# Fewer and wider idle products on TensorE

## The chip, the core and the metric

The kernel runs on one core of a Trainium2 chip. The metric is the device time of one execution in microseconds. A core has five engines, each with an instruction queue of its own: TensorE (PE, matrix products; its weight loads are PEld), VectorE (DVE), ScalarE (ACT), GpSimd (POOL) and SyncE (SP, which issues most loads and stores). They wait for each other by semaphores.

## The reference

Attention over 4 batches and 8 heads of 768 positions and 64 columns, then a gated two-layer network on the 3072 rows of 512. Heads marked for retrieval see all earlier positions; the others see the first 4 and the last 64.

```python
scores = scale * np.matmul(q, k.transpose(0, 1, 3, 2))
mask = np.where(retr[0, :, 0, 0, None, None], full_mask, stream_mask)
scores = np.where(mask[None, :, :, :], scores, -1000000000.0)
a = np.exp(scores - np.max(scores, axis=-1, keepdims=True))
a = a / (np.sum(a, axis=-1, keepdims=True) + 1e-09)
x = np.matmul(a, v)            # then heads side by side: 3072 x 512
h = x @ w_in                   # 512 -> 2048
g = h * (1.0 / (1.0 + np.exp(-beta * h)))
out = g @ w_out                # 2048 -> 512
```

## The kernel before

The work is cut into eight units, one for each batch and half of the positions (384 rows). For a unit, queries and keys are loaded, cast to bf16 (tiles `c`), turned on TensorE against the identity (`transposes_of`, in the first two units one tensor and pair of heads at a time), copied to `QK`, multiplied to scores (`scores`, into PSUM tiles `sp`), passed through the exponential on ScalarE (tiles `es`, or `osb`) and masked. Sums of the exponentials and their products with v follow, the sums are inverted and spread, and the result `xT` (512 rows, 384 columns) goes through the network: `w_in`, a tanh form of the gate, `w_out`, a copy out of PSUM and a store.

All operations of all units are in one list, and `SEQUENCE` is the order in which they are issued, so each engine gets its instructions in that order. Loads go through SP's queue. The network of one unit runs beside the attention of the next, which keeps TensorE full from about 20 us on; before that only the first unit's attention is there.

In this first stretch the kernel issues idle products: matrix products whose results nobody reads, into PSUM that real work overwrites afterwards. `FILLS` names operations of the list by number and says how many idle products are issued ahead of the real ones; `fill_first` issues 25 at the very start. Operation 28 turns the first keys, 32 and 36 the keys of the second and fourth pair of heads; 45, 51, 54 and 60 are scores; 24 is the product that makes the rows of the first positions (`sink_rows`). The operand `blank` is a cleared piece of an `xT` tile, cleared on VectorE by the first instruction there. Ahead of transposes the PSUM tile is bf16, and there the idle product is a transpose of the identity.

```python
FILLS = {24: 4, 28: 8, 32: 1, 36: 1, 45: 5, 51: 7, 54: 5, 60: 1}
for i, f, e in plan.run():
    held["fill"] = FILLS.get(i, 0)
    f(e)
```

Of the kernel before, what the change touches and what calls it, by code (L numbers as in the profile page):

```python
# [8 lines left out]
F32 = mybir.dt.float32  # L9
BF16 = mybir.dt.bfloat16  # L10
# [9 lines left out]
NQ = 384  # L20
# [85 lines left out]
    return bass.AP(ap.tensor, ap.offset + offset, [list(ap.ap[0])] + dims)  # L106


FILLS = {24: 4, 28: 8, 32: 1, 36: 1, 45: 5, 51: 7, 54: 5, 60: 1}


class _Ordered:
# [60 lines left out]
def kernel(  # L173
# [14 lines left out]
    pe, dve, act, pool, sp = (_Ordered(tc, e) for e in (nc.tensor, nc.vector, nc.scalar, nc.gpsimd, nc.sync))  # L188
# [3 lines left out]
    NP = len(PAIRS)  # L192
# [4 lines left out]
    def tpool(name, bufs, space=None):  # L197
        kw = {} if space is None else {"space": space}
        return ctx.enter_context(tc.tile_pool(name=name, bufs=bufs, **kw))
# [11 lines left out]
    xp = tpool("xp", RINGS["xT"])  # L211
# [4 lines left out]
    ps = tpool("ps", 1, PSUM)  # L216
    dp = tpool("dram", 2, bass.MemoryType.DRAM)

    def bank(name):
        return ps.tile([128, 512], F32, name=f"b{plan.where['b', name]}")  # L220

    def banks(name):
        return ps.tile([128, 2, 512], F32, name=f"sp{plan.where['sp', name]}")
# [7 lines left out]
    ident = consts.tile([128, 128], BF16, name="ident")  # L231
# [11 lines left out]
    sel_c = consts.tile([128, 2, 8], F32, name="sel_c")  # L243
    sel_k3 = consts.tile([128, CK // 2], F32, name="sel_k3")
    low = consts.tile([128, 1], F32, name="low")
    blank = xp.tile([128, NP, NQ], BF16, name="xT")[:, 0, 0:128]
    one = consts.tile([128, 63], BF16, name="one")
    warm = consts.tile([128, 1], F32, name="warm")
    QK = [consts.tile([128, 2, NP, S], BF16, name=f"QK{par}") for par in range(2)]
# [216 lines left out]
    held = {}  # L466

    def sink_rows(b):

        t = bank((2 * b, "k"))  # L470
        fill(t[:, 0:128])
        pe.matmul(t[0:96, :], sink_sel, v_b[b][:, 0, :, :].rearrange("p h d -> p (h d)"), start=True, stop=True)
        held["sinks"] = t

# [53 lines left out]

    def fill(dst):
        for _ in range(held["fill"]):  # L530
            if dst.dtype == BF16:
                pe.transpose(dst, ident, ident)
            else:
                pe.matmul(dst, blank, blank, start=True, stop=True)

    def fill_first():
        held["fill"] = 25
        fill(bank("fill")[:, 0:128])

    def transposes(x, pi):  # L540
        t = ps.tile([128, 2, 512], BF16, name=f"b{plan.where['b', (x.n, 'T', pi)]}")
# [11 lines left out]
    def transposes_of(x, pi, i):  # L553
        t = ps.tile([128, 2, 512], BF16, name=f"b{plan.where['b', (x.n, 'T', pi, i)]}")
        x.ps["T", pi, i] = t[:, 0, 0:NQ].rearrange("p (t n) -> p t n", t=TU)
        c = x.ld[pi, "c"]
        fill(x.ps["T", pi, i][:, 0, :])
        for t in range(TU):
            pe.transpose(x.ps["T", pi, i][:, t, :], c[:, i, t * 128:(t + 1) * 128], ident)

# [122 lines left out]
    def piece(x, h, a, n):  # L683
        for (c, w, e) in x.work[h]:
            if c <= a and a + n <= c + w:
                return e[:, a - c:a - c + n]

    def scores(x, pi, ri, mixed=None):
# [5 lines left out]
        if lent(pi, ri, x.n):  # L694
            ps = [bank((x.n, pi, ri, i)) for i in range(2)]
        else:
            both = banks((x.n, pi, ri))
            ps = [both[:, i, :] for i in range(2)]
        if x.n == 0:
            fill(ps[0][:, 0:128])  # L700
        ops = [[], []]
        last = []
        nb, ne = NE[u] // SINK, NE[u]
# [7 lines left out]
        for i, half in enumerate(rounds[ri]):  # L711
            if half is None:
                continue
            if half[0][0] == "k":
                for g in range(NP):
                    p = min(g, NP - 2) + 1
# [36 lines left out]
            for h in dict.fromkeys(t[1] for t in half if t[0] in "sw"):  # L753
                pieces = [t for t in half if t[0] in "sw" and t[1] == h]
                q0 = 0 if pieces[0][0] == "w" else pieces[0][4]
                n = NQ if pieces[0][0] == "w" else sum(t[5] for t in pieces)
# [23 lines left out]
    def scores_mixed(x, bu):  # L780

        todo = []
        for pi, ri in bu:
            scores(x, pi, ri, todo)
        queues = {}
        for o in [o for r in todo for o in r]:
            row, col = (a.offset // a.ap[0][0] for a in (o[1], o[0]))
            queues.setdefault((row, col), []).append(o)
        at = dict.fromkeys(queues, 0)
        while queues:  # L790
            g = min(queues, key=lambda g: at[g])
            o = queues[g].pop(0)
            n = 1
            for d in o[2].ap[1:]:
                n *= d[1]
            at[g] += max(n, 64) + 6
            pe.matmul(o[0], o[1], o[2], start=True, stop=True)
            if not queues[g]:
                del queues[g]
# [86 lines left out]
    def sink_from(u):  # L886
        return 2 * W if u == 0 else 0
# [4 lines left out]
    def sums(x, part):  # L892
        if part == 0:
            x.sm = bank((x.n, "s"))
            if x.n == 0:
                fill(x.sm[:, 0:128])
        todo = [[] for _ in range(4)]
        heads = [h for pi in SUMS[part] for h in PAIRS[pi]]
        for c in range(CK):
            a = c * W  # L900
            g, s = PLACE[c]
            for h in heads:
                e8 = two[:, 1, 31 - h:63 - h] if c >= 4 else two[:, 0, 31 - 16 * s - h:63 - 16 * s - h]
                if RETR[h]:
                    todo[g] += [(e8, e[:, a - q0:a - q0 + W]) for (kb, q0, n, e) in x.work[h] if q0 <= a // 128 * 128 < q0 + n]
                else:
                    todo[g].append((e8, piece(x, h, a, W)))
            if part == len(SUMS) - 1 and a >= sink_from(x.u):
                todo[g].append((esel_k[:, 16 - 16 * s:48 - 16 * s], x.esk[0:96, a:a + W]))
        for r in range(max(len(w) for w in todo)):  # L910
            for g in range(4):
                if r < len(todo[g]):
                    l, e = todo[g][r]
                    pe.matmul(x.sm[32 * g:32 * g + 32, 0:W], l, e, start=(part == r == 0),
                              stop=(part == len(SUMS) - 1 and r == len(todo[g]) - 1))
# [105 lines left out]
    def moved(x, h):  # L1021
        return x.u and h == 6

    def pv(x, g):
        vb = v_b[x.b]
        ve = VE[x.b]
        o = banks((x.n, "v", g))
        if x.n == 0:
            fill(o[:, 0, 0:128])
        ops = [[], []]  # L1030
        nb = NE[x.u] // SINK
        for t in (2 * g, 2 * g + 1):

            for i, h in enumerate(XT[t] if x.n else (2 * t, 2 * t + 1)):
                dst = o[i * D:(i + 1) * D, t - 2 * g, :]
                todo = ops[i]
                if h in x.zero:
                    todo.append((W, dst[:, 0:W], x.vz[:, h, :] if h < H // 2 else x.vs[:, 0, h, :], x.zero[h], t, 0))
                if RETR[h]:

                    cut = 256 if moved(x, h) else NQ
                    for (kb, q0, n, e) in x.work[h]:
                        a = min(max(cut - q0, 0), n)
                        if a:
                            todo.append((a, dst[:, q0:q0 + a], vb[:, kb, h, :], e[:, 0:a], t, 0))
                        if a < n:
                            ops[1 - i].append((n - a, o[(1 - i) * D:(2 - i) * D, t - 2 * g, NQ + q0 + a - cut:NQ + q0 + n - cut],
                                               vb[:, kb, h, :], e[:, a:n], t, 0))
                else:
                    q0 = sink_from(x.u)  # L1050
                    for m in range(1 if h in x.zero else 0, CK):
                        if x.n < 2 and m * W == q0:
                            todo.append((NQ - q0, dst[:, q0:NQ], ve[0:96, h - 1, :], x.esk[0:96, q0:NQ], t, 0))
                        mg = CK * x.u + m
                        l = vb[:, (mg - 1) // 2, h, :] if mg % 2 else x.vs[:, m // 2, h, :]
                        todo.append((W, dst[:, m * W:(m + 1) * W], l, piece(x, h, m * W, W), t, int(x.n < 2 and not mg % 2)))
                    if x.n < 2:
                        continue
                    todo.append((NE[x.u], dst[:, 0:NQ].rearrange("d (c n) -> d c n", n=W)[:, CK - nb:, 0:SINK], ve[:, h - 1, :], x.edge[h], t, 0))
        todo = []  # L1060
        for late in range(2):
            at = [0, 0]
            queue = [[o for o in ops[i] if o[5] == late] for i in range(2)]
            while queue[0] or queue[1]:
                i = min((i for i in range(2) if queue[i]), key=lambda i: at[i])
                todo.append((i, *queue[i].pop(0)))
                at[i] += todo[-1][1]
        for k, (i, n, a, l, r, t, _) in enumerate(todo):
            same = [j for j, w in enumerate(todo) if w[0] == i and w[5] == t]
            pe.matmul(a, l, r, start=k == same[0], stop=k == same[-1], skip_group_check=True)  # L1070
        x.ps["v", g] = o
# [362 lines left out]
# [3 lines that stand above are left out]
# [35 lines left out]
```

## Time and profile before

| what | value |
|---|---|
| runs of the kernel | 229.29 us median of 3 (228.82 to 229.96) |
| span of the profiled execution, first to last instruction | 227.1 us |
| outside the span, median less span | 2.2 us |
| TensorE busy | 220.0 us, 97% of the span |
| ScalarE, VectorE, GpSimd busy | 144.4, 152.0, 97.1 us |
| mean granted clock of TensorE | 0.999 |

The runs were timed without the profiler, and the profiled execution has no time of its own beside its span; so the span is set against the median. A busy row of the profile gives when an instruction started and how long it took up to its modelled end; matrix products overlap, so the distance of their starts is the rate and the length is more than that. Names that the profile shows are those of tiles, without buffer numbers: `b` and `sp` are PSUM tiles, `c` the cast queries and keys, `xT` both the network's input and the idle operand, `ident` the identity. All instructions carry line 123, that of a helper, so they are told apart by their tiles.

### The profile page before, as it was taken

How to read it: one execution, taken by the hardware profiler on the slowest of the kernel's cores; microseconds unless marked ns; L12 is line 12 of the kernel's file. 1: busy time of each engine (PE TensorE's matmuls, PEld its weight loads, DVE VectorE, ACT ScalarE, POOL GpSimd, SP SyncE). 2: the span in 40 equal slices, each digit the busy share in tenths (PEclk: the TensorE clock that was granted, in tenths of full speed). 3: DMA queues.
4: the chain of work that ended last, by engine and by line, in shares of the span. 5: the costliest groups of instructions: out<-in, count | busy, mean ns of one | idle time of the engine just before them, and what ended most of it. 6: DMA issues, size and time to landing. Idle time of an engine off the chain costs nothing.

```text
span 227.1 us, 6564 instructions
## 1 busy us (share of the span) xinstructions
PE 220.0 (97%) x2595; PEld 127.2 (56%) x2595; DVE 152.0 (67%) x391; ACT 144.4 (64%) x244; POOL 97.1 (43%) x238
## 2 busy tenths in 40 slices
PE   7688999999999999999999999999999999999995
PEld 7564567664545565555654665465655555456543
DVE  5787988888292878856862668983796864157700
ACT  6899979886447488616786198318965665118620
POOL 5528966965978108749566293042800000000000
PEclk9999999999999999999999999999999999999999
DMA  6999999998999969999999996947801027021012
GB/s 185 283 321 369 242 343 349 371 335 217 233 205 244 213 131 235 270 176 208 267 219 189 202 214 192 219 26 178 188 0 46 4 89 200 3 92 46 3 46 92
DMA packets 84264, 42.28 MB, mean 186 GB/s; under 512 B 66042, under 2 KB 77002, under 8 KB 84234
## 3 DMA queue, kind: packets, MB, share of 16 engines
q1 hardware_dynamic: 83962, 41.67, 76.7%
q8 instruction: 20, 0.33, 0.6%
q10 hardware_dynamic: 272, 0.20, 0.3%
q14 instruction: 10, 0.08, 0.1%
HBM read 32.27 MB, written 6.37 MB: 170 GB/s over the span
## 4 chain that ended last, share of the span: by engine, by line
PE 87%; DMA 5%; DVE 3%; ACT 2%; SPq 1%; issue 1%; POOL 0%; ACTq 0%
PE b L123 77%; PE sp L123 10%; DMA vf<-in_v_dram 3%; DMA q2f<-in_q_dram 2%; DVE gT L123 1%; ACT t L123 1%; SPq L123 1%; ACT R L123 1%; DVE vs L123 1%; DVE xT L123 0%; ACT vb L123 0%; DVE QK L123 0%; POOL c L123 0%; DVE b L123 0%; DVE lo L123 0%
## 5 line engine op out<-in xcount | busy, mean ns | idle before, releaser
L123 PE MATMUL b<-xT,w_in 128*128 128x384 bf16 x512 | 89.9, 326 | 0.1
L123 PE MATMUL b<-w_out,gT 128*128 128x512 bf16 (+2 forms) x400 | 88.3, 371 | 0.0
L123 DVE SCALAR_TENSOR_TENSOR gT<-t,b 128x384 bf16<-128x384 f32 x128 | 68.5, 551 | 26.2 <-ACT t L123 22.5
L123 ACT ACTIVATE t<-b,beta_h 128x384 f32<-128x384 f32 x128 | 72.2, 586 | 18.3 <-PE b L123 9.7
L123 PEld LDWEIGHTS <-w_in 128*128 128x128 bf16 x512 | 48.6, 98 | 33.4 <-issue 0.6
L123 PEld LDWEIGHTS <-gT 128*128 128x128 bf16 x400 | 37.4, 98 | 40.9 <-issue 0.8
L123 ACT ACTIVATE es<-sp 128x1024 bf16<-128x1024 f32 (+2 forms) x44 | 41.2, 961 | 6.5 <-PE sp L123 6.0
L123 ACT ACTIVATE osb<-b 128x512 f32<-128x512 f32 (+1 forms) x18 | 10.5, 583 | 34.7 <-PE b L123 34.7
L123 DVE TENSOR_TENSOR xT<-sp,R 64x384 bf16<-64x384 f32 (+4 forms) x31 | 16.6, 554 | 12.2 <-PE sp L123 9.2
L123 POOL CAST c<-wf 128x256 bf16<-128x256 f32 x48 | 20.7, 473 | 7.6 <-DMA wf<-in_k_dram 7.4
L123 POOL COPY KP<-QK 128x24 bf16<-128x24 bf16 (+5 forms) x41 | 9.9, 286 | 27.1 <-DMA QK<-c 16.6
L123 PE MATMUL sp<-QK 64*64 64x128 bf16 (+6 forms) x360 | 14.9, 240 | 0.9 <-ACT QK L123 0.8
L123 DVE TENSOR_TENSOR es<-es,mask_s 128x128 bf16<-128x128 bf16 (+8 forms) x34 | 13.0, 402 | 3.8 <-ACT es L123 3.6
L123 PEld LDWEIGHTS <-QK 64*64 64x64 bf16 (+1 forms) x432 | 10.8, 106 | 7.2 <-issue 4.9
L123 DVE TENSOR_TENSOR es<-es,mask_c 128x128 bf16<-128x128 bf16 (+3 forms) x42 | 10.4, 272 | 6.2 <-ACT es L123 6.1
L123 POOL CAST vb<-wf 128x512 bf16<-128x512 f32 x18 | 11.2, 629 | 7.9 <-DMA wf<-in_v_dram 7.8
L123 PE MATMUL sp<-es,vb 128*64 128x64 bf16 (+5 forms) x245 | 13.0, 233 | 0.3 <-ACT es L123 0.3
L123 ACT COPY sc<-b 128x384 f32<-128x384 f32 x5 | 2.4, 479 | 15.7 <-PE b L123 15.7
L123 DVE TENSOR_SCALAR osb<-b 128x512 f32<-128x512 f32 (+1 forms) x7 | 4.7, 667 | 11.3 <-PE b L123 11.3
L123 PEld LDWEIGHTS <-vb 128*64 128x64 bf16 x257 | 11.6, 111 | 0.7 <-issue 0.3
L123 POOL CAST w_in<-wf 128x512 bf16<-128x512 f32 x16 | 9.4, 624 | 4.7 <-DMA wf<-in_moe_w_in_dram 4.6
L123 DVE COPY QK<-b 128x384 bf16<-128x384 bf16 (+1 forms) x13 | 8.2, 640 | 4.8 <-PE b L123 4.7
(120 smaller groups left out, 212.1 us busy)
## 6 DMA issues: line engine op xcount, KB each, us to landing
out_dram<-osb SPq DMA_DIRECT2D x23, 256.0 KB, 3.6
wf<-in_v_dram SPq DMA_DIRECT2D x18, 256.0 KB, 5.3
wf<-in_moe_w_in_dram SPq DMA_DIRECT2D x4, 1024.0 KB, 8.5
wf<-in_moe_w_out_dram SPq DMA_DIRECT2D x4, 1024.0 KB
R<-rd SPq DMA_DIRECT2D x9, 384.0 KB, 5.7
q2f<-in_q_dram SPq DMA_DIRECT2D x16, 192.0 KB, 4.1
wf<-in_q_dram SPq DMA_DIRECT2D x12, 256.0 KB, 4.0
wf<-in_k_dram SPq DMA_DIRECT2D x12, 256.0 KB, 3.8
```

Source lines behind the costliest of these rows:

```text
L123: ins = f(*a, **k)
```

## The change

The idle operand becomes 512 columns wide, with 128 of them as weights, and an idle product streams all 512. The counts are about a fourth: 25 become 6, and `FILLS` goes from 4, 8, 1, 1, 5, 7, 5, 1 to 1, 2, 0, 0, 1, 2, 1, 0 in the order of its keys. 57 products of 128 columns become 13 of 512, 7296 columns in all become 6656. Ahead of transposes the idle product is now a matrix product too, into the same PSUM tile read as fp32. No operation changes its place.

```diff
-FILLS = {24: 4, 28: 8, 32: 1, 36: 1, 45: 5, 51: 7, 54: 5, 60: 1}
+FILLS = {24: 1, 28: 2, 45: 1, 51: 2, 54: 1}
...
-    blank = xp.tile([128, NP, NQ], BF16, name="xT")[:, 0, 0:128]
+    blank = xp.tile([128, NP, NQ], BF16, name="xT").rearrange("p a n -> p (a n)")[:, 0:512]
...
     def fill(dst):
         for _ in range(held["fill"]):
-            if dst.dtype == BF16:
-                pe.transpose(dst, ident, ident)
-            else:
-                pe.matmul(dst, blank, blank, start=True, stop=True)
+            pe.matmul(dst, blank[:, 0:128], blank, start=True, stop=True)
 
     def fill_first():
-        held["fill"] = 25
-        fill(bank("fill")[:, 0:128])
+        held["fill"] = 6
+        fill(bank("fill"))
...
-        fill(x.ps["T", pi, i][:, 0, :])
+        fill(t.rearrange("p a n -> p (a n)").bitcast(F32))
...
-            fill(ps[0][:, 0:128])
+            fill(ps[0][:, 0:512])
```

The other callers of `fill` (`sink_rows`, `sums`, `pv`) hand over the whole tile in the same way.

On TensorE's queue, at the end of the opening: before, the last of the 25, the eight transposes of the identity (the first and the last shown), then the first real transpose, which reads a cast tile `c`.

```order
L123 MATMUL b_144<-xT 128x128
L123 LDWEIGHTS ident [waits Pool_49]
L123 MATMUL b_221<-ident 128x128
...
L123 MATMUL b_221<-ident 128x128
L123 LDWEIGHTS c [waits Activation_49]
L123 MATMUL b_221<-ident,c 128x128
```

After, at the same place:

```order
L123 MATMUL b_144<-xT 128x512
L123 LDWEIGHTS xT
L123 MATMUL b_202<-xT 128x512
...
L123 MATMUL b_202<-xT 128x512
L123 LDWEIGHTS c [waits Activation_49]
L123 MATMUL b_202<-ident,c 128x128 [waits Pool_49]
```

The idle work ahead of the first transposes no longer reads the identity, so the wait for GpSimd, which builds it, has gone from the idle product to the first real transpose.

On TensorE's queue at operation 60, the second scores of the last pair of heads, before:

```order
L123 MATMUL b_393<-ident,c 128x128
L123 LDWEIGHTS xT
L123 MATMUL sp_398<-xT 128x128 [waits Activation_49]
L123 LDWEIGHTS QK_109
L123 MATMUL sp_398<-QK_109 64x256
```

And after:

```order
L123 MATMUL b_353<-ident,c 128x128
L123 LDWEIGHTS QK_109
L123 MATMUL sp_358<-QK_109 64x256 [waits Activation_49]
```

The idle product is gone, and its wait for the PSUM tile to be read by ScalarE stands at the first real product.

More of the change, by code (lines that the diff above doesn't have):

```diff
@@ L470, in sink_rows @@
         t = bank((2 * b, "k"))
-        fill(t[:, 0:128])
+        fill(t)
         pe.matmul(t[0:96, :], sink_sel, v_b[b][:, 0, :, :].rearrange("p h d -> p (h d)"), start=True, stop=True)
@@ L895, in sums @@
             if x.n == 0:
-                fill(x.sm[:, 0:128])
+                fill(x.sm)
         todo = [[] for _ in range(4)]
@@ L1028, in pv @@
         if x.n == 0:
-            fill(o[:, 0, 0:128])
+            fill(o[:, 0, :])
         ops = [[], []]
```

## The prediction

> **What bounds the kernel now.** I read the page first: the busy line, the slices and the chain that ended last.
>
> ```profile
> span 227.1 us, 6564 instructions
> PE 220.0 (97%) x2595; PEld 127.2 (56%) x2595; DVE 152.0 (67%) x391; ACT 144.4 (64%) x244; POOL 97.1 (43%) x238
> ...
> PE   7688999999999999999999999999999999999995
> ...
> PE 87%; DMA 5%; DVE 3%; ACT 2%; SPq 1%; issue 1%; POOL 0%; ACTq 0%
> ```
>
> TensorE bounds the kernel: 97% busy, and 87% of the chain. But the slices are 5.7 us each, and the first three (7, 6, 8 tenths) are the only ones before the last where it is not full. The idle products lie exactly there, so the second view is the timeline of TensorE alone over the first 14 us. The columns are start, length, what ran, how often, and in brackets the idle time before it with its releaser.
>
> ```profile
> 1.06 2.85 PE L123 MATMUL b<-xT 128*128 128x128 bf16 x25 [1.06 <-DVE xT L123]
> 3.71 1.06 PE L123 MATMUL b<-ident 128*128 128x128 bf16 x8
> 4.82 0.52 PE L123 MATMUL b<-ident,c 128*128 128x128 bf16 x6
> 5.17 0.44 PE L123 MATMUL sp<-xT 128*128 128x128 bf16 x5
> 5.90 0.50 PE L123 MATMUL sp<-QK 64*128 64x384 bf16 x6 [0.29 <-ACT QK L123]
> ...
> 7.57 0.51 PE L123 MATMUL b<-ident,c 128*128 128x128 bf16 x6 [0.89 <-ACT c L123]
> 7.91 0.22 PE L123 MATMUL b<-ident 128*128 128x128 bf16 x1
> 7.97 0.33 PE L123 MATMUL b<-ident,c 128*128 128x128 bf16 x3
> 8.27 0.55 PE L123 MATMUL sp<-xT 128*128 128x128 bf16 x7
> 9.34 0.55 PE L123 MATMUL sp<-QK 64*64 64x128 bf16 x20 [0.52 <-ACT QK L123]
> ...
> 10.35 0.22 PE L123 MATMUL b<-ident 128*128 128x128 bf16 x1
> 10.50 0.34 PE L123 MATMUL b<-ident,c 128*128 128x128 bf16 x3
> 10.88 0.44 PE L123 MATMUL sp<-xT 128*128 128x128 bf16 x5
> 11.41 0.36 PE L123 MATMUL sp<-QK 64*64 64x128 bf16 x12
> ...
> 12.12 0.22 PE L123 MATMUL sp<-xT 128*128 128x128 bf16 x1
> 12.27 0.35 PE L123 MATMUL sp<-QK 64*64 64x256 bf16 x4
> 12.55 0.35 PE L123 MATMUL sp<-QK,KP 128*32 128x384 bf16 x4
> 12.83 0.40 PE L123 MATMUL b<-xT 128*128 128x128 bf16 x4
> 13.06 0.38 PE L123 MATMUL b<-vb,KP 128*96 128x512 bf16 x1
> ```
>
> The idle products are all rows that read xT, and the rows that read ident alone: 25, 8, 5, 1, 7, 1, 5, 1 and 4, together 57. The gaps behind them end on ScalarE (ACT c, ACT QK), so TensorE waits there for others. Who sets the end in this stretch is told by the third view, the chain in order of time:
>
> ```profile
> 2.33 4.23 DMA q2f<-in_q_dram
> ...
> 7.31 6.58 DMA vf<-in_v_dram
> ...
> 13.91 0.63 ACT vb L123
> ...
> 17.18 0.49 PE b L123 x4
> ```
>
> From 2.33 to 13.89 us the path is two loads with 0.75 us between them, then a cast on ScalarE. The first TensorE instructions that stand in it are the four at 17.18 us (the spread of the reciprocals). What the change does before 13.9 us therefore reaches the end only if it makes TensorE late for somebody, or if it changes TensorE's clock.
>
> **The price of one idle product.** Starts tell the rate, since the lengths hold the drain as well. The 25 take (3.71 - 1.06) / 25 = 0.106 us each; from 4.82 on six take (5.17 - 4.82) / 6 = 0.058 us. The clock doubles between. The groups by shape, for 3.6 to 4.7 us and for 4.81 to 5.45 us, say the same by their means:
>
> ```profile
> L123 PE MATMUL b<-ident 128*128 128x128 bf16 x8 | 1.1, 311 | 0.0
> ...
> L123 PE MATMUL b<-ident,c 128*128 128x128 bf16 x6 | 0.5, 222 | 0.1
> ```
>
> A mean of 311 ns falls to 222 ns. The granted clock of the page shows 1.00 here and does not see this step, so I go by the starts.
>
> A product of 512 columns is not among the idle ones of before; by columns I take four narrow ones, 4 x 0.106 = 0.43 us slow and 4 x 0.056 = 0.22 us at full clock (0.055 to 0.058 in the rows). Were a product priced by the piece, it would be 0.06 to 0.11; were it a serial one of twice that, 0.45 and 0.85. The first is nearest, since slow and fast rows both scale with the clock as streaming does.
>
> **The change part by part.** The memset that clears the operand grows from 64 to 256 words in each partition. Its own row and the one nearest in size are:
>
> ```profile
> L123 DVE MEMSET xT<- 128x64 uint32 x1 | 0.1, 112 | 0.9 <-PEq L1453 0.9
> ...
> L123 DVE MEMSET VE<- 128x224 uint32 x1 | 0.2, 245 | 0.1
> ```
>
> (245 - 112) / 160 = 0.83 ns a word, so 256 words take about 272 ns and the first product starts 0.16 us later, at 1.22; bounds are 0 and 0.34 (four times 112 ns). On VectorE it costs nothing, since that engine waits 0.63 us for the identity soon after:
>
> ```profile
> 1.81 0.45 DVE L123 TENSOR_REDUCE sel_c<-ident 128x8 f32<-128x64 bf16 x2 [0.63 <-POOL ident L123]
> ```
>
>
> The opening: 25 + 8 narrow products become 6 + 2 wide ones. Before, 33 x 0.1065 = 3.51 us from 1.06, done at 4.57; after, 8 x 0.426 = 3.41 us from 1.22, done at 4.63. The next real product, the first transposes at 4.82, waits for a cast on ScalarE that starts at 4.25 and takes 0.51:
>
> ```profile
> 4.25 0.51 ACT L123 CAST c<-k2f 128x384 bf16<-128x384 f32 x1 [0.26 <-DMA k2f<-in_k_dram]
> ...
> 6.59 0.51 ACT L123 CAST c<-q2f 128x384 bf16<-128x384 f32 x1 [0.73 <-DMA q2f<-in_q_dram]
> ```
>
> So the cover is 4.82 - 4.63 = 0.19 us, and with the dearest memset 0.01. Cost: 0.
>
> The four other places that keep idle products: five at 5.17 (0.28) become one (0.22), with the next real product at 5.90; seven at 8.27 (0.39) become two (0.45), done at 8.72, with the next at 9.34 held by ACT QK; five at 10.88 become one, next at 11.41; four at 12.83 (0.23) become one (0.22), next at 13.06. Even at the slow clock the two at 8.27 would end at 8.27 + 0.85 = 9.12, before 9.34. Cost: 0, plus or minus 0.06.
>
> The three places that lose their one idle product: at 7.91 it takes 0.06, at 10.35 up to 0.15 (next 10.50, which waits for a cast anyhow), at 12.12 0.15. TensorE gets at most 0.36 us back. Only the last one lies in front of work that is ready: the scores behind it end near 12.55 + 0.35 = 12.90 and would end at 12.75. Whoever reads them earlier still meets the load that lands at 13.89, a microsecond later. Taken: 0; bounds -0.36 and 0.
>
> Sum: 0 - 0 - 0 against the profiled span of 227.1 us. The runs of before are 228.82, 229.29 and 229.96, so the median stands 2.2 us above the span; launch and end are in it and nothing here touches them. Forecast 229.3 us, the median.
>
> **The rivals.** First, the clock, which decides on the other side. The idle products keep TensorE at work in a thin stretch, and the end of the trace shows that its clock is cut when it rests:
>
> ```profile
> 222.91 1.38 PE L123 MATMUL b<-w_out,gT 128*128 128x384 bf16 x18
> ...
> 226.00:226.70 0.70, 0.00 (x0) 1.00 0.00 0
> 226.70:227.10 0.40, 0.00 (x0) 0.55 0.00 0
> ```
>
> The first row is the last work of TensorE, over at 224.29. The other two are stretches (length, PE busy, granted clock): still 1.00 up to 226.70, 0.55 after, so the cut comes at about 226.74, 2.45 us after the last product. The longest gap at the start is 0.89 us (at 7.57), and by my sums no gap grows by more than 0.15. A gap of 0.89 us is survived and one of 2.45 is not; 0.89 is the nearest, so I expect the clock to hold. By density it reads the same. These are stretches of 3.4 us with TensorE's busy time, the last of them ending at the cut:
>
> ```profile
> 4.87:8.29 3.42, 2.25 (x31) 1.00 1.01 317
> 8.29:11.70 3.41, 2.76 (x55) 1.00 1.25 248
> ...
> 223.33:226.74 3.41, 0.96 (x17) 1.00 0.23 77
> ```
>
> After 0.96 us of work in the last one the clock was cut. After 2.25 in the first it was not, as the spacing at 8.27 and later is still 0.055. The change takes 0.06 and 0.06 from that stretch, to 2.13, and about 0.2 from the second. Should the limit lie between 2.13 and 2.25, or should the stretches fall otherwise in another run, TensorE would go at half clock through one such stretch: of 2.76 us of work 1.7 would be done, 1.05 us late; in a full stretch 1.7 late. ScalarE is fed by it, so no load hides this. That gives 230.3 to 231.0, and 230.7 in the middle; slower by 0.5% it is from 1.15 us on. Chance 0.12.
>
> [...]
>
> [...] The time by this rule is the one of the clock's rival, 230.3 to 231.0, and of its chance 0.12 I give it 0.04.
>
> Second rival: the freed 0.36 us reach the end after all, since TensorE is the bound later on. That gives 228.9. For it speaks the 97% busy; against it, that the chain has none of TensorE's work until 17 us. Chance 0.13.
>
> Third rival: the idle products get in the way. If the memset takes 0.45 us, and the wide products a tenth more than four narrow ones, the opening ends at 1.40 + 3.75 = 5.15 and the transposes start 0.33 late. ScalarE's copy of their result waits for them, but its next cast waits 0.73 us for a load until 6.59, so most of it is swallowed: 229.3 to 229.6. Chance 0.10.
>
> **How the numbers follow.** No reach to the end: 0.60; freed products 0.13; in the way 0.10; clock 0.12; something not seen, 0.05. All but the clock lie within 0.5% of 229.29 (228.14 to 230.44), about what a measurement of this kernel can tell from no change. The clock's 0.12 is slower in about 0.09, the unseen is split: faster 0.05, same 0.83, slower 0.12. The range takes in the freed products with the scatter of the runs shown, 0.5 us below, and the clock's middle above: 228.4 to 230.8.
>
> **What would show it.** In the trace after: 13 idle products of 512 columns, 0.43 us apart up to about 4.6 us and 0.22 later; first product at about 1.2; first transposes still at 4.8; the load of v landing at 13.9 and the chain from there as before; product spacing of 0.056 at 8.3 and 10.9. If transposes between 5 and 14 us have means near 311 ns, the clock was lost and I am wrong by that rival. If the spread at 17.2 comes more than 0.3 us earlier or later, the zero in the sum is wrong.

## The result, and the profile after

The changed kernel takes 236.68 us (median of 4 runs, 235.28 to 237.14). The kernel before takes 229.1 us in the runs beside it (228.82 to 229.96). The ratio is 1.029, with an interval of 1.026 to 1.033: slower by 7.6 us, and outside the forecast range. Executions more than 1.5% longer than the fastest of the same kernel are in the medians given here, but not in the ratios.

First the page of the changed kernel; its profiled execution took 235.28 us, with a span of 233.6 us, 6.5 us more than the span before.

```profile
span 233.6 us, 6476 instructions
...
PE 221.6 (95%) x2551; PEld 125.3 (54%) x2551; DVE 155.3 (66%) x391; ACT 144.8 (62%) x244; POOL 96.7 (41%) x238
...
PEclk9799999999999999999999999999999999999999
...
PE 83%; DVE 6%; ACT 4%; issue 2%; DMA 2%; SPq 1%; ACTq 0%
```

Three things are new. The granted clock shows a 7 in the second slice. "Issue", time in which an engine waits for nothing that the profile shows, has risen from 1% to 2% of the chain. VectorE's share of the chain has doubled, from 3% to 6%. The first is the rival that I had priced. The second I had not thought of, and it is the largest loss; the third belongs to the loss at 60 us, below.

The opening, in the timelines of VectorE (one row) and of TensorE, is as forecast.

```profile
0.94 0.27 DVE L123 MEMSET xT<- 128x256 uint32 x1 [0.94 <-PEq L1450]
```

```profile
1.26 3.59 PE L123 MATMUL b<-xT 128*128 128x512 bf16 x8 [1.26 <-DVE xT L123]
4.65 0.58 PE L123 MATMUL b<-ident,c 128*128 128x128 bf16 x6
...
7.02 0.34 PE L123 MATMUL b<-ident,c 128*128 128x128 bf16 x3 [0.72 <-DVE c L123]
8.12 1.09 PE L123 MATMUL b<-ident,c 128*128 128x128 bf16 x9 [0.76 <-ACT c L123]
9.00 1.06 PE L123 MATMUL sp<-xT 128*128 128x512 bf16 x2
```

The memset takes 0.27 us, the eight wide products are (4.65 - 1.26) / 8 = 0.42 us apart, and the first transposes start at 4.65. Then the clock: three windows of 3.4 us (length, PE busy, PEld, DVE, ACT and POOL busy, granted clock, DMA share, GB/s; in brackets the number of instructions).

```profile
4.80:8.21 3.41, 1.58 (x19) 0.88 (x18) 1.80 (x6) 1.55 (x4) 0.38 (x1) 1.00 1.00 317
8.21:11.63 3.42, 3.42 (x40) 2.46 (x41) 2.34 (x5) 3.15 (x6) 2.25 (x9) 0.50 1.15 240
11.63:15.04 3.41, 3.10 (x79) 1.48 (x77) 3.05 (x9) 3.28 (x7) 1.01 (x4) 1.00 0.89 288
```

After a window with 1.58 us of work the next one ran at 0.50. The transposes show it too; from 8.3 to 11.4 us their mean is near the 311 ns that the prediction had named as the sign of a lost clock:

```profile
L123 PE MATMUL b<-ident,c 128*128 128x128 bf16 x15 | 1.9, 303 | 0.8 <-ACT c L123 0.8
```

But set the same real product of both kernels side by side, and call the difference of their starts the lag. It is 0.68 us at 6.34 us of the kernel before, when the clock has not yet been cut (VectorE's cast of a piece of the queries waited for its load until 6.60 us; before, it started at 5.85). It is 0.94 us at 10 us, and 0.8 us from 20 up to 32 us. Of 6.5 us the cold window explains some 0.3.

At 32.97 us of the kernel before the lag jumps to 4.51. The chain of waits, there:

```profile
33.49 0.54 PE sp L123 x6
34.03 3.44 issue
37.48 2.05 PE sp L123 x42
```

The stretches around it, of the changed kernel and then of the kernel before:

```profile
34.00:36.00 2.00, 0.03 (x1) 0.00 (x0) 1.58 (x5) 0.58 (x1) 2.00 (x4) 1.00 1.05 379
36.00:38.00 2.00, 0.52 (x9) 0.47 (x10) 0.00 (x0) 0.00 (x0) 1.12 (x3) 1.00 1.09 346
```

```profile
34.00:36.00 2.00, 2.00 (x42) 1.79 (x39) 1.66 (x5) 1.95 (x5) 1.78 (x5) 1.00 1.05 360
36.00:38.00 2.00, 2.00 (x15) 1.20 (x13) 2.00 (x5) 1.75 (x6) 0.70 (x2) 1.00 1.09 339
```

TensorE stands still for 3.44 us in the middle of full work, at a place that the change does not touch, and the profile shows no engine, no semaphore and no load that releases it. What it waits for is in the DMA section of the page, which reads the same before and after. Below it stands the only such packet of the changed kernel between 25.2 and 36.3 us, in a window from 35.1 to 36.3, as its row of the queues.

```profile
q8 instruction: 20, 0.33, 0.6%
```

```profile
q8 instruction: 1, 0.02, 5.2%
```

Queue q8 brings TensorE's instructions by these counts: 0.33 MB in 20 transfers of 16 KB, 256 instructions each, as the run with +168 shows below, and the 2551 products and 2551 weight loads of the page are 19.9 times 256. In all eight standstills of this document one of them lands 1.3 to 1.4 us before TensorE resumes. The third goes from 35.18 to 36.17 us, and TensorE resumes at 37.48. In the kernel before it starts at 25.93 us, long before it is needed. Up to its standstill TensorE had done this (products and weight loads):

```profile
0.00:34.50 34.50, 29.70 (x479) 17.02 (x480) 26.84 (x83) 28.50 (x50) 21.38 (x59) 0.95 0.94 284
```

479 + 480 = 959 records. In the kernel before the 959th is passed at 31.4 us without a stop.

The rest of the loss comes at 60 us (before: 55.3 us), where sums of the exponentials, dense before, now wait for VectorE:

```profile
60.02 0.19 PE L123 MATMUL b<-es,one_z 128*32 128x64 bf16 x1
60.62 0.19 PE L123 MATMUL b<-es,one_z 128*32 128x64 bf16 x1 [0.41 <-DVE es L123]
61.52 0.21 PE L123 MATMUL b<-es,one_z 128*32 128x64 bf16 x2 [0.70 <-DVE es L123]
```

There the lag goes to 6.48. So: 0.8 up to 32 us, 3.7 by the standstill, 2.0 at 60 us, 6.5 in all.

VectorE is late there because its products of the exponentials with the masks take longer. Five of the thirteen, after and then before:

```profile
57.36 1.61 DVE L123 TENSOR_TENSOR es<-es,mask_s 128x256 bf16<-128x256 bf16 x3
58.89 0.97 DVE L123 TENSOR_TENSOR es<-es,mask_c 128x64 bf16<-128x64 bf16 x2
```

```profile
52.95 0.69 DVE L123 TENSOR_TENSOR es<-es,mask_s 128x256 bf16<-128x256 bf16 x3
53.56 0.32 DVE L123 TENSOR_TENSOR es<-es,mask_c 128x64 bf16<-128x64 bf16 x2
```

The thirteen take 2.4 us more in all. Now GpSimd's casts run beside them. The first of these casts, after and then before:

```profile
56.30 0.51 POOL L123 CAST c<-q2f 128x384 bf16<-128x384 f32 x1 [2.75 <-DMA q2f<-in_q_dram]
```

```profile
55.62 0.51 POOL L123 CAST c<-q2f 128x384 bf16<-128x384 f32 x1 [2.71 <-DMA q2f<-in_q_dram]
```

Before, the masks end at 55.1 us, ahead of the casts. After, TensorE and with it VectorE are 4.4 us late, the casts, which wait for loads, only 0.7 us, and so the masks (57.16 to 61.9) fall among them.

### The profile page after: what moved, and what is told of

Same layout as the page of the kernel before. It is cut to its first block, busy times and chain, and to the rows that moved or that the text cites. A ratio compares the mean times of both kernels' runs of the same rounds, so it can differ in the third digit from the quotient of the medians.

```text
span 233.6 us, 6476 instructions
## 1 busy us (share of the span) xinstructions
PE 221.6 (95%) x2551; PEld 125.3 (54%) x2551; DVE 155.3 (66%) x391; ACT 144.8 (62%) x244; POOL 96.7 (41%) x238
## 4 chain that ended last, share of the span: by engine, by line
PE 83%; DVE 6%; ACT 4%; issue 2%; DMA 2%; SPq 1%; ACTq 0%
PE b L123 73%; PE sp L123 10%; DVE gT L123 2%; ACT t L123 2%; DMA q2f<-in_q_dram 2%; DVE es L123 2%; DVE KP L123 1%; ACT osb L123 1%; ACT es L123 1%; SPq L123 1%; DVE vs L123 1%; ACT QK L123 0%; ACT c L123 0%; DVE QK L123 0%; ACT vb L123 0%
## 5 line engine op out<-in xcount | busy, mean ns | idle before, releaser
L123 POOL CAST c<-wf 128x256 bf16<-128x256 f32 x48 | 19.6, 448 | 11.8 <-DMA wf<-in_k_dram 11.3
L123 DVE TENSOR_TENSOR es<-es,mask_s 128x128 bf16<-128x128 bf16 (+8 forms) x34 | 15.1, 462 | 4.3 <-ACT es L123 4.1
L123 DVE TENSOR_TENSOR es<-es,mask_c 128x128 bf16<-128x128 bf16 (+3 forms) x42 | 11.3, 294 | 6.1 <-ACT es L123 6.0
L123 POOL COPY vs<-vb 64x512 bf16<-64x512 bf16 x19 | 11.3, 626 | 0.3
```

The lines of the kernel that those rows point to most:

```text
L123: ins = f(*a, **k)
```

## The experiments

The theories: the loss comes from the number of TensorE's instructions ahead of the dense work (where the fetched block ends), or from the clock, or from the wide products being in the way. The diffs are against the changed kernel and show the lines that matter. `PADS` counts "tiny" idle products, issued after the others; `held["n"]` is the number of columns. A tiny idle product has 32 columns of weights and streams 4 columns, so it adds two instructions (product and weight load) and next to no columns. Counts of instructions are against the kernel before, in which the change removes 88.

**Four kernels that take the change apart.** First, the opening as before (25 and 8 narrow products), the later ones wide, and 19 tiny products, so that the count is that of before (0):

```diff
-FILLS = {24: 1, 28: 2, 45: 1, 51: 2, 54: 1}
+FILLS = {24: 1, 28: 8, 45: 1, 51: 2, 54: 1}
+PADS = {24: 3, 32: 1, 36: 1, 45: 4, 51: 5, 54: 4, 60: 1}
...
-        held["fill"] = 6
+        held["fill"], held["n"], held["pad"] = 25, 128, 0
```

> Opening of before (25 + 8 narrow), later idle products wide as in the change (1, 2, 1, 1), and 19 tiny products of 4 columns beside them, so that TensorE has exactly as many instructions ahead of each real product as before. Columns between 4.8 and 14 us are those of the change. Theory clock (the thin stretch loses the clock, and all else follows from that): cold stretches as after the change, mean clock 0.978 to 0.993, 234 to 237 us. Theory fetch (fewer instructions ahead move the points at which TensorE's instructions are fetched, and it runs dry near 34 us): no gap of 3 us at 34, 229 to 231 us, even if a stretch is cold.

The second is the whole change with seven more wide products at the later places (-74):

```diff
-FILLS = {24: 1, 28: 2, 45: 1, 51: 2, 54: 1}
+FILLS = {24: 1, 28: 2, 32: 1, 36: 1, 45: 3, 51: 3, 54: 2, 60: 1}
```

> The change with more wide products at its own places (32, 36, 60: 1 each; 45: 3; 51: 3; 54: 2), 7 more in all, so the early stretch is denser than before the change; still 74 TensorE instructions fewer than before. Theory clock: no cold stretch, 229 to 230 us. Theory fetch: clock full, but the gap of 3 to 4 us near 33 us stays, 232 to 235 us.

The third has only the opening wide (-50; the later products have 128 columns), the fourth only the later places (-38):

```diff
-FILLS = {24: 1, 28: 2, 45: 1, 51: 2, 54: 1}
+FILLS = {24: 4, 28: 2, 32: 1, 36: 1, 45: 5, 51: 7, 54: 5, 60: 1}
...
+        held["fill"], held["n"] = FILLS.get(i, 0), 512 if i == 28 else 128
```

> Only the opening wide (6 + 2), the later idle products narrow and as many as before (plain products in place of transposes). 50 TensorE instructions fewer than before. Theory clock: density as before, clock full, 229 to 230 us. Theory fetch: somewhere between, 229 to 234 us, with a gap near 33 us if 50 instructions are enough to move the fetch behind the loads.

```diff
-FILLS = {24: 1, 28: 2, 45: 1, 51: 2, 54: 1}
+FILLS = {24: 1, 28: 8, 45: 1, 51: 2, 54: 1}
...
-        held["fill"] = 6
+        held["fill"], held["n"] = 25, 128
```

> Only the later idle products wide and fewer (24: 1, 45: 1, 51: 2, 54: 1), opening narrow as before (25 + 8). 38 TensorE instructions fewer than before. Theory clock: cold stretches as after the change, 234 to 237 us. Theory fetch: 229 to 234 us; against the padded kernel of the same columns it is slower by the gap near 33 us, 3 us, if 38 instructions are enough.

| kernel | instructions | median us | ratio to before | standstill after record 959 |
|---|---|---|---|---|
| opening narrow, tiny added | 0 | 229.65 | 1.001 [0.997, 1.004] | none |
| only later places wide | -38 | 229.36 | 1.000 [0.997, 1.003] | none |
| only opening wide | -50 | 234.47 | 1.020 [1.014, 1.026] | 1.9 us |
| denser later places | -74 | 235.26 | 1.024 [1.018, 1.029] | 2.5 us |
| the change | -88 | 236.68 | 1.029 [1.026, 1.033] | 3.8 us |

(The last column is the distance of two starts on TensorE.) The order is that of the count. It is not that of the clock: the kernel with the opening alone had the full clock in every run and lost 5 us; the one with the later places alone was profiled with a cold window (mean clock 0.993) and took 229.36 us. The chain of the kernel with the opening alone:

```profile
31.23 1.22 PE b L123 x110
32.44 1.67 issue
34.11 1.05 PE b L123 x12
```

**Is it the count?** The whole change and 44 tiny products (0), and the opening alone with 6 tiny products at operation 51 (-50 becomes -38):

```diff
+PADS = {24: 2, 32: 2, 36: 2, 45: 13, 51: 13, 54: 10, 60: 2}
```

> The whole change, and 44 products of 4 columns beside its later idle products, so that TensorE again has as many instructions ahead of each later real product as before the change. Theory fetch (runs so far: TensorE runs dry after 959 of its products and weight loads whenever the third fetch of its instructions starts after 31 us; with 50 fewer instructions ahead it is asked for after a load of 2 MB): no gap near 33 us, third fetch before 29 us, 229 to 230.5 us. Theory clock: cold stretches stay, since 176 columns add nothing, 234 to 237 us.

```diff
+PADS = {51: 6}
```

> The kernel with only the opening wide (234.5 us, 50 instructions fewer than before, full clock), and six products of 4 columns more at operation 51: 38 fewer, as in the kernel with only the later ones wide (229.4 us). Theory fetch: twelve instructions decide, 229 to 230.5 us and no gap. Against it, a theory that the wide opening itself costs 5 us: 234 to 235 us as without them.

Both are as fast as before: 229.47 us, ratio 0.9995 [0.997, 1.002], and 230.2 us, 1.002 [0.999, 1.005]. Twelve instructions that do nothing take away 4 us. Two of the ten executions of the second took 235.1 and 236.6 us; with -38 the margin may be small, but neither was profiled. Two of the ten of the first took 237.1 and 257.6 us, at mean clocks of 0.964 and 0.853. The longer one is the profiled one, and only the absence of a standstill is read from it.

**Is the fetch late because of loads?** In the changed kernel the third fetch runs among 2 MB of loads. One load of 1 MB was issued later, after operation 179; then, in another kernel, nine loads, from operation 517 on, were held back behind a small store that waits for the gate's result.

```diff
-    ... 550, 128, 553, 522, 144, ... 134, 146, 179, 561, ...
+    ... 550, 128, 553, 144, ... 134, 146, 179, 522, 561, ...
```

> The change with one line of the order moved: the load of the last quarter of w_out (1 MB) is issued after seven loads of queries and keys of unit 2 rather than ahead of six of them. TensorE's instructions are those of the change, so nothing is different for the clock. Theory fetch: the third fetch stands behind 1 MB less, at some 390 KB a us 2.7 us earlier, so the gap near 33 us shrinks from 3.8 to about 1 us and the time to 231 to 234 us. Theory count alone (the point of the fetch in the program, whatever is loaded): 236 to 237 us.

```diff
+            gate = dp.tile([96, 64], BF16, name="gate")
+            sp.dma_start(out=gate, in_=units[0].gT[0:96, 7, 0:64])
...
+    ... 133, 566, 517, 522, 171, 175, 165, 173, 167, 177, 179, ...
```

> The change with the burst of nine loads (two of 1 MB among them) held back on SP's queue by a small store that waits for the eighth piece of gT (about 29.9 us; the burst began at 28.0). TensorE's instructions and idle products are those of the change. Theory fetch behind loads: the third fetch, asked for near 28.8 us, finds a short queue, starts by 30.5 us and no gap of more than 1 us is at product 959; the later weights may cost time elsewhere, 230 to 235 us. Theory count alone: gap of 3 to 4 us as after the change.

Both missed the standstill that they forecast (about 1 us, and at most 1 us). The four executions of the first took 233.3, 237.3, 237.6 and 239.5 us, at mean clocks of 1.000, 0.986, 0.986 and 0.978, so no ratio is read from them. The profiled one is that of 233.3 us. It lies in the range of the fetch theory, but by luck: its standstill is 3.4 us, and the time is shorter because its real products run 0.7 us ahead of the kernel before up to the standstill and because nothing is lost at 60 us. The second took 237.05 us, 1.033 [1.026, 1.039], standstill 3.7 us. Its transfers are nearly idle from 29.5 to 31.5 us, and the fetch did not use that time; it started at 34.78 (window columns as above):

```profile
29.50:31.50 2.00, 2.00 (x63) 0.99 (x61) 1.75 (x4) 2.00 (x6) 2.00 (x4) 1.00 0.27 25
31.50:33.50 2.00, 2.00 (x111) 1.45 (x98) 1.83 (x4) 1.06 (x3) 0.05 (x1) 1.00 0.84 306
```

By this the fetch was not asked for near 28.8 us, as I had assumed. But the theory that it waits among loads does not fall with that. In the kernels without a standstill the third fetch starts near TensorE's record 690 (see below). Here that record runs at 31.13 us, after the two loads of 1 MB were issued (30.11 and 30.60), and from there to the start of the fetch the transfers are full again (share 0.98). The first kernel does not test it either: between its record 690 and the fetch the share is 1.05.

**What are the idle products worth?** All 57 kept in number, each of 4 columns (0):

```diff
-            pe.matmul(dst, blank[:, 0:128], blank, start=True, stop=True)
+            pe.matmul(dst[:, 0:4], blank[:, 0:128], blank[:, 0:4], start=True, stop=True)
```

> All 57 idle products kept in number but of 4 columns, so the instruction stream is that of before and the idle products keep the clock up no longer. Theory fetch: no gap near 33 us; the cost is only the cold clock up to some 12 us, of which the wait for loads hides most: 229 to 231 us, mean clock at most 0.99. Theory clock: 234 us or more.

233.43 us, ratio 1.0145 [1.009, 1.020], which is 3.3 us: slower than I expected. There is no standstill at record 959, but the full clock is first recorded at 19.41 us, and the transposes up to 13 us have a mean of 305 ns. The same products run 2.4 us later at 17 us, 2.0 later from 20 to 45, and 4.1 at the end. What the products stream does matter. About 2 us of it arise where the clock is slow; the other 2 come at 50 us and between 70 and 100 us, at full clock, and were not traced. The change keeps the streaming.

**The change once more**, for a second profile.

> The change unaltered, for a second profile. Theory fetch: TensorE runs dry again after the same 959 products and weight loads, for 2.5 to 4 us near 33 us, with a third fetch that starts after 31 us. If a cold stretch is to be seen beside the early one, it begins within 3.5 us of the end of that gap: the gap itself costs the clock. Theory clock: cold stretches lie before 20 us only, and the gap's place moves with them.

236.83 us, standstill 3.73 us, again after 959 records. This execution has no cold window early; it has one directly behind the standstill:

```profile
34.06:37.47 3.41, 0.24 (x4) 0.21 (x5) 1.35 (x4) 0.40 (x1) 2.55 (x5) 1.00 1.05 363
37.47:40.88 3.41, 3.41 (x53) 3.15 (x50) 0.00 (x0) 1.55 (x4) 3.01 (x10) 0.50 1.07 283
```

Here the standstill fills a window (0.24 us of work in 3.41), the next one runs at 0.50, and the lag grows from 4.26 to 5.74 us within that window.

**Block ends, or fewer instructions?** Two kernels tell whether the place of a block's end decides. The first has more idle products than any other, +168 instructions, which is 88 short of one block of 256:

```diff
+PADS = {24: 9, 32: 5, 36: 5, 45: 14, 51: 14, 54: 12, 60: 6}
...
-        held["fill"] = 6
+        held["fill"], held["pad"] = 3, 66
```

> More idle products than ever: three wide ones and 66 of 4 columns in the opening, then the change's wide ones and 65 of 4 columns at the places of before; TensorE gets 168 instructions more than in the kernel before, which is 88 fewer than a whole block of 256 more. Theory A (TensorE fetches its instructions in blocks of 256, and what counts is where the block's end falls in the work): the work stands to the block ends as in the changed kernel, so TensorE runs dry again for 3 to 4 us near 33 to 34 us, now after 959 + 256 = 1215 recorded products and weight loads, and the time is 233 to 238 us. Theory B (fewer instructions as such make the fetch late; more of them give it time): no gap, 229 to 231 us. Theory C (the fetch was late for other reasons, such as the loads): no gap tied to a record number; 229 to 238 us.

It took 239.0 us, ratio 1.035 [1.028, 1.042]. Its windows and chain:

```profile
0.00:38.40 38.40, 36.75 (x607) 22.52 (x608) 26.43 (x79) 28.58 (x49) 25.03 (x64) 1.00 0.97 292
```

```profile
37.92 0.54 PE sp L125 x6
38.45 3.99 issue
42.44 1.63 PE sp L125 x27
```

607 + 608 = 1215 = 959 + 256, at the same place of the work. Adding instructions brought the standstill back; taking them away had made it. The time is 1 us above what I gave. In the profiled execution, of 241.3 us, the real products are 1.1 to 1.8 us late by 10 us and 5.0 to 5.3 from 17 us up to the standstill, since the full clock is first recorded at 23.16 us: its many tiny products stream little, as in the kernel above.

In the second, the 44 tiny products stand behind the first unit's work, at the second unit's products with v (count 0 for the kernel, -88 up to record 945):

```diff
+PADS = {161: 22, 163: 22}
...
-        if x.n == 0:
+        if x.n <= 1:
             fill(o[:, 0, :])
```

> The whole change, and 44 products of 4 columns, so that TensorE has as many instructions as in the kernel before; but they stand behind the work of the first unit, 22 at each of the two products with v of the second unit (from about the 945th record), where TensorE runs dry in the changed kernel. Theory A (the place of the block's end in the work ahead of it decides): the first 940 records are those of the changed kernel, so TensorE runs dry after 959 for 3 to 4 us; the blocks behind it end where they do in the kernel before, so the second loss at 55 to 61 us (about 1.5 us) goes: 232.5 to 236.5 us. If the second loss is only the first one's echo, 235 to 237 us. Theory B (the whole count decides): 229 to 230.5 us.

238.1 us, ratio 1.037 [1.032, 1.043].

```profile
0.00:32.90 32.90, 28.05 (x479) 15.87 (x480) 25.84 (x80) 27.98 (x49) 20.68 (x57) 1.00 0.98 290
```

```profile
32.70 0.26 PE sp L125 x7
32.95 4.28 issue
37.23 2.81 PE sp L125 x32
```

The total count of before does not help; dry after 959 again. I missed the time: the standstill is longer, the clock is then cut for two windows (34.63 to 41.46 us), and the 22 tiny products stand in dense work. The lag is 7.84 before the second loss, which here is only 0.3 us.

**How long a block lasts.** The 256 records ahead of the standstill, 703 to 959, are by that spacing the last block that TensorE has before it runs dry. The time they take, in the kernel before, with only the later places wide, the opening alone with and without 6 tiny products, the change, +168 (there 959 to 1215), and the tiny ones behind; each row is one kernel's, in this order:

```profile
26.96:31.42 4.46, 4.46 (x131) 2.56 (x132) 3.68 (x8) 4.46 (x10) 4.16 (x7) 1.00 0.93 268
```

```profile
28.59:32.08 3.49, 3.48 (x137) 2.16 (x131) 2.88 (x5) 3.49 (x8) 2.47 (x5) 1.00 0.96 332
```

```profile
29.16:32.57 3.41, 3.41 (x136) 2.08 (x131) 2.67 (x5) 3.41 (x8) 2.95 (x5) 1.00 0.87 256
```

```profile
29.52:32.26 2.74, 2.56 (x130) 1.63 (x128) 2.53 (x6) 2.74 (x7) 0.78 (x2) 1.00 1.04 383
```

```profile
31.45:33.71 2.26, 2.26 (x138) 1.71 (x138) 2.06 (x5) 1.40 (x3) 0.46 (x1) 1.00 1.04 392
```

```profile
35.88:38.13 2.25, 2.25 (x137) 1.70 (x137) 2.19 (x4) 1.18 (x3) 2.25 (x4) 1.00 1.10 344
```

```profile
30.65:32.80 2.15, 2.15 (x138) 1.65 (x138) 1.94 (x5) 1.40 (x3) 0.46 (x1) 1.00 1.02 371
```

(The windows include the neighbours of the 256 at both edges.) No standstill at 4.46, 3.49 and 3.41 us; standstills of 1.9, 3.8, 4.3 and 4.4 us at 2.74, 2.26, 2.25 and 2.15. In these kernels it is a threshold more than a scale: the denser kernel passes the 256 in the shortest time, 2.0 us, and stands for only 2.5. The reason for the short times is in the changed kernel's timeline:

```profile
31.40 1.12 PE L123 MATMUL b<-es,two 128*32 128x64 bf16 x107
```

The sums run 107 products of 64 columns in 0.9 us (31.40 to 32.32), that is 214 instructions. In the kernel before this run begins near record 772, inside the block, behind 3.7 us of slower work; with -88 it begins near 684, ahead of the block's beginning, and TensorE races through nearly the whole block. The fetch itself takes 1.0 to 1.2 us of transfer in the kernels that stand still, and 1.3 to 1.4 us more go by from its landing to the first product.

The block is read from the traces: 0.33 MB / 20 is 16 KB, and 1215 - 959 is 256 records. Its end was crossed without a standstill where the 256 took 3.41 us or more, and with one where they took 2.74 us or less. In seven of the eight standstills the fetch started only 0.2 to 2.0 us after TensorE had started its last record, so there it did not run while the block was executed.

What stays open: why the fetch starts late. No record shows the moment of the request. The third fetch starts 0.9 us before to 0.6 us after record 690 in the kernels without a standstill and 3.2 to 4.2 us after it in those with one (with +168: the fourth fetch, and record 946). The standstill comes mostly from these 3 to 4 us. In the changed kernel 2.3 us go by from record 690 to the last one before the standstill, and transfer and resumption take 2.3 us; a fetch that started at record 690 would, by this estimate, hardly have been missed. Two explanations are left. The request may come late, for a reason that no run shows. Or the request may come in time and wait among the loads: in all eight profiles with a standstill the transfers are full between record 690 and the fetch (share 0.98 to 1.11), and the fetch starts 4.7 us or more after the first of the two 1 MB loads was issued; in the six without one it starts at most 1.0 us after that. No run separates the two.

The loss at 60 us follows the masks and the casts in the profiles. In the kernels with -50 to -88 in which it appears (1.4 to 2.5 us), masks run beside GpSimd's casts. Where loads were moved, the casts begin at 58.47 us, behind the last mask at 58.07, and nothing is lost there, although the standstill is 3.4 us; with +168 the masks begin at 63.98, when the casts are over; with the tiny ones behind, three masks are longer and 0.3 us is lost. With 4 columns it went the other way: the masks kept their length and one cast took 1.58 us instead of 0.51. So by these profiles the standstill brings this loss only where it moves the masks among the casts. No run was made that moves the casts alone.

## Why the prediction was wrong

**Where it failed.** The step is "What the change does before 13.9 us therefore reaches the end only if it makes TensorE late for somebody, or if it changes TensorE's clock." It lacks a third way: TensorE gets its instructions in blocks (16 KB a transfer, 256 records from 959 to 1215), and 88 fewer of them move every later piece of work against the blocks' ends. What the runs showed in its place is a standstill of 3.7 us after record 959, and 2.0 us more where the lateness moved VectorE's masks among GpSimd's casts. The sum priced products by time alone ("Cost: 0" for each place) and gave their two instructions no place in the stream. The loss came 20 us after the last idle product (13.69 us), where no part of my sum looks. By the text it falls under "something not seen", 0.05; it should have had a name, since the row of queue q8 stood in the page before.

**The first rival, the clock.** It happened, and its sign, transposes near 311 ns, was seen: 2.25 us of work in 3.41 held the clock, 1.58 us lost it. But busy time alone does not decide it, as the prediction took it to: a window with 1.46 us (35.52 to 38.94 of the changed kernel) held the clock, and one with 1.95 us (6.79 to 10.21 of the kernel with the gate) lost it. The forecast of 2.13 us for that window was too high, mostly since the transposes came later with their loads (7.02 and 8.12 instead of 6.34 and 7.57) and fell in part outside it. The size, 1.05 to 1.7 us for one cold window, was too high here: early in the changed kernel a window cost 0.3 us. Runs of the kernel before show one too: in the last comparison the two at 0.993 took 230.88 and 230.65 us, the five at 1.000 229.61 in the mean, 1.2 us less; in the two comparisons with 19 runs each the difference is 0.9 and 0.6 us. So it is neither special to the change nor its cause. Alone it would have left the time in the forecast range. No run shows the rule to which I gave 0.04 of this rival's 0.12; what the runs showed in its place is the cold window of 3.42 us behind 1.58 us of work, worth 0.3 us.

**The second and third rivals.** The freed 0.36 us did not show at the end. The idle products were not in the way either: memset 0.27 against 0.272 us, wide products 0.42 against 0.426 us apart at the slow clock, first transposes at 4.65 against 4.82 before. The kernel with only the later places wide came out at 1.000, so the costs of 0 there were right.

**What would have shown it.** "If the spread at 17.2 comes more than 0.3 us earlier or later, the zero in the sum is wrong": it came at 18.30, 1.1 us late. But the two kernels at -38 and -50 differ by 12 instructions and 4 us, and no reading of the first 18 us tells that.

No version beat both kernels. The whole change with its 44 tiny products equals the kernel before, and what the idle products stream is worth some 3 us in either form.

## What to carry to other kernels

An instruction that does nothing still has a place in its engine's stream. When a change adds or removes instructions ahead of a dense run of short ones, count records to that run, compare them with the block ends (here 959 and 1215), and look for a wait on "issue" with an instruction-queue packet behind it; here twelve tiny idle instructions took the standstill of 1.9 us away, and 4 us with it. A delay of one engine can cost a second time where it moves its work, or another engine's, beside work that it did not meet before; here it was 2.0 us behind a standstill of 3.7. Judge such a change at the dense run behind it, not where it was made.

## What the runs showed of the hardware that I had not expected

- TensorE ran dry after 959 records in seven profiles of six kernels, and after 1215 in one with 256 - 88 more; the standstill was 1.9 to 4.4 us.
- A standstill of 3.7 us in one execution halved the clock for the next 3.41 us, and one of 4.4 us for 6.83 us; the 3.8 us in the first profile of the change did not.
- VectorE's mask products took 0.5 to 0.6 us instead of 0.2 to 0.3 beside GpSimd's casts; once the masks kept their length and a cast of 0.51 us took 1.58.
- 57 idle products of 4 columns instead of 128 delayed the first full clock to 19.41 us and cost 3.3 us.
